# Logits inside the turn of each output tile, routing in separately planned instructions, and a plan with traced durations

## The chip, the cores and the metric

The kernel runs on 1 core of one Trainium2 chip. The metric is the device time of one execution in microseconds (us), as the median of several runs. The profile and the trace are those of one execution, taken by the hardware profiler.

Names of engines: PE is TensorE (PEld its weight loads), DVE is VectorE, ACT is ScalarE, POOL is GpSimd, SP is SyncE, which here only issues DMAs. L12 is line 12 of the kernel before.

## What is computed

Three layers, one after the other, in float32. The first is a gated linear attention with a complex, per-element decay; the second a mixture of 8 experts, of which each token takes one (top-1, with a capacity of 384 per expert); the third a dense FFN with a leaky ReLU. Cut to what matters:

```python
# q, k, v, a_re, a_im: (2, 8, 768, 48); the state S is 48x48 complex per head
for t in range(768):
    S = a[t] * S + outer(k[t], v[t])      # |a| is limited to 0.999
    y[t] = q[t] @ real(S)
x = y as (1536 tokens, 384)

logits = x @ w_gate                        # (1536, 8)
e = argmax(logits); gate = softmax(logits)[e]
slot = number of earlier tokens with the same e    # kept while slot < 384
out = gate * (relu(x @ w1[e]) @ w2[e])     # w1: 8 x 384 x 1024, w2: 8 x 1024 x 384

h = out @ w_in                             # 384 -> 2048
return (max(h, 0) + alpha * min(h, 0)) @ w_out     # 2048 -> 384
```

## The kernel before

**The front part.** The 1536 tokens are 12 tiles of 128. For each tile the decay is brought into log-polar form, summed along the tokens by a matmul with a triangle (`log_polar`, `decay`, `turns`, `edge`), turned back into factors, and multiplied into keys and queries (`rotate`). `attend` (L608 to L740) then works per tile with all 8 heads: it transposes keys and queries, four heads at a time (L628, PSUM tag `tr`, two buffers), copies them out (L633 on ScalarE, L635 on VectorE), forms the scores (L648), masks them on VectorE (L654), and forms the output `y` (L667) and the state update `u` (L681). The output comes out with features on the partitions, two heads of 64 padded rows side by side. ScalarE copies it to `xT` (L701); four transpositions per tile turn it to tokens on the partitions, in a PSUM tile `px` that shares the two `tr` buffers (L706); and ScalarE copies the 48 real columns per head out as the rows `x` (L710).

**Routing.** `route(g)` (L743) works on groups of tiles: `ROUTES` is [0, 1, 2], [3, 4, 5], [6, 7], [8, 9], [10, 11]. For each tile `logit` forms the logits with four matmuls from `xT` and `wg` into a PSUM tile `lg` (L763). `choose` (L774 to L790) is one block of VectorE instructions: the largest logit, its first index, a one-hot row in bf16, the difference to the largest, and, per tile, a copy of the running counts `racc` and an addition to them. `count` (L792) forms the slots with three small bf16 matmuls. `place` (L800 to L823) is a second block: the slot of each token, whether it is over capacity, the index of its row for the scatter (`sidx`) and for the later gather (`gidx`), five instructions that prepare the first FFN tiles (`eidx`), and a part of the gate. GpSimd then scatters the rows to HBM with an indirect DMA per tile (`send`, L840). The last group, [10, 11], is not planned: `first_expert` (L878 to L949) writes its instructions out in order, between warming matmuls (L1112), the product `pa` (L920) that assembles the first expert's tokens without waiting for the scatter of the last tiles, and the halves `xh`, `xl` of it (L939, L940). `finish_routes` (L951) takes the exponentials and finishes the gates.

**The order.** All instructions of the front part but those of `first_expert` are put in order by a planner, `Plan` (L86). Each step has an engine, a cost in us, the values it reads and writes, and PSUM or SBUF buffers that it needs. The planner goes through time, and on each engine takes next what can start earliest, ties by `rank` (a number per kind of step plus the tile's index, table `RANK`) and then by the longest remaining path. `LAG` is added from one step's end to the start of those that depend on it. Steps with `port=True` on VectorE and GpSimd are kept from overlapping each other. Before `COLD` us the planner takes TensorE's steps as `SLOW` times as long; before `EARLY` us DMA issues as `HEAVY` times as long. The order found is fixed per engine; each engine then works it off strictly in turn and waits by semaphores. `choose` and `place` are one step each, with costs of 1.2 + 0.25 n and 1.3 to 2.0 us for n tiles.

**Filling.** Where the plan shows a gap on TensorE longer than `FILL_MIN` ahead of a step that has a `fill`, 0.6 of that gap (`FILL`) is filled with matmuls on the triangle (`keep_warm`, L1110 to L1112), whose result is overwritten. They start once the triangle, part of the load `cst`, has landed.

**Behind the front part** come 8 experts of 256 tokens (`ffn`: `hp` at L1194, `y` at L1177, with each f32 operand split into a high and a low half and three products of these) and the FFN on three chunks of 512 tokens. The splitting of weights (`wh` on ScalarE, `wl` on VectorE) runs beside. Two experts' first weights are split in the front part (L1016, L1020) where the plan finds room.

Of the kernel before, what the change touches and what calls it, by code (L numbers as in the profile page):

```python
# [189 lines left out]
def const_array():  # L190
# [5 lines left out]
    for c in range(2):  # L196
# [4 lines left out]
    io = np.tile(np.arange(NE), (P, GT))  # L201
    c = np.concatenate(
        [tri, tri / (2 * math.pi), last, tri - np.eye(P), cq, ck, io, twin, np.eye(P), np.tile(np.arange(SLOTS), (P, 1))],
# [6 lines left out]
def tile_kernel(  # L210
# [34 lines left out]
    iota = consts[:, CW + P:CW + P + SLOTS]  # L245
    xh0 = cpool.tile([P, DM // P, SLOTS], F32R, name="xh0")
# [112 lines left out]
    wg = acp.tile([P, H // 2, NE], F32, name="wg")  # L359
# [24 lines left out]
    plan = Plan({**RAW, **TMP, "kk": TMP["qq"], "v": 6, "x": 6, "kT": 2, "qT": 2, "pT": 2, "xT": GT, "st": 3, **PS}, ("tr", "sc"))  # L384
# [31 lines left out]
    def load(g, names, cost=0.6):  # L416
        for i in groups[g]:
            for nm in names:
# [9 lines left out]
                plan.op("S", cost, fn, put=[f"{nm}{i}"], new=[(nm, f"{nm}{i}")], lag=2.2)  # L428
# [56 lines left out]
    def decay(i):  # L485
# [6 lines left out]
        tensor(0.65, lambda: T.matmul(out=pl(), lhsT=tri, rhs=tl[f"l{i}"], start=True, stop=True),  # L492
# [7 lines left out]
    def edge(i):  # L500
# [21 lines left out]
        tensor(0.26, turn, use=[e0, "ident"], put=[p], new=[("pc", p)])  # L522
        vector(0.08, lambda: V.tensor_copy(out=ze(), in_=pz()[:, :, 31]), use=[p], put=[f"ze{i}"])
        tensor(0.2, spread, use=[f"ze{i}", "cst"], put=[p])
# [6 lines left out]
    def turns(i):  # L531
# [8 lines left out]
        tensor(0.65, lambda: T.matmul(out=pl(), lhsT=tri_pi, rhs=tl[t], start=True, stop=first),  # L540
               use=[t, "cst"], put=[p], new=[("pc", p)], fill=lambda: pl()[:, 0:P])
        if not first:
            tensor(0.65, lambda: T.matmul(out=pl(), lhsT=last_row, rhs=tl[f"f{i - 1}"], start=False, stop=True),  # L543
                   use=[f"f{i - 1}"], put=[p])
# [63 lines left out]
    def attend(i):  # L608
# [12 lines left out]
        def tr(hh):  # L621
            for src, nm, sc in ((kk, "kT", 1.0 / LAM), (qq, "qT", 1.0)):
# [14 lines left out]
                tensor(0.45, turn, use=[src, "ident"], put=[p], new=[("tr", p), (nm, t)],  # L637
# [22 lines left out]
        def outs(hh):  # L660
            def products():
# [12 lines left out]
                new=[] if hh else [("y", f"y{i}")],  # L674
            )

        def state(hh):
# [8 lines left out]
            tensor(0.7, products, use=[kk, vk], put=[f"u{i}"], new=[] if hh else [("u", f"u{i}")])  # L686
# [13 lines left out]
        def out():  # L700
            A(out=buf(wk, "xT", xk, [P, H // 2, P], GT), in_=y(), func=ACTF.Copy)  # L701

        def back():
            pt = psum("tr", p, [P, H // 2, P])
            for j in range(H // 2):
                T.transpose(pt[:, j, :], tl[xk][:, j, :], ident)  # L706

        def rows():
            xt[i] = xpool.tile([P, DM], F32, tag="x", name="x", bufs=6)
            A(  # L710
                out=xt[i].rearrange("p (h d) -> p h d", d=D),
                in_=tl[p].rearrange("p j (m d) -> p (j m) d", d=HW)[:, :, 0:D], func=ACTF.Copy,
            )
# [29 lines left out]
    def route(g):  # L743
# [8 lines left out]
        def bank(shape, key, tag):  # L752
            return psum(tag if tail else "u", key, shape)

        for j, i in enumerate(tl_):
            x = f"xT{i}"
            if tail:
                plan.rank = i - 1

            def logit(j=j, x=x):  # L760
                pl = bank(shp, f"lg{g}", "sc")
# [116 lines left out]
    def first_expert():  # L878
# [69 lines left out]
        for j in range(n):  # L948
            V.tensor_tensor(out=racc, in0=racc, in1=ohb[:, j], op=ALU.add)  # L949
# [592 lines left out]
```

## Time and profile before

| | us |
|---|---|
| median of 3 runs | 526.89 (525.55 to 528.17) |
| the profiled execution's own time | 525.41 |
| its span, first to last instruction | 523.4 |
| TensorE busy, share of the span | 497.0 (95%) |
| VectorE busy | 352.5 (67%) |
| ScalarE busy | 307.5 (59%) |
| GpSimd busy | 70.1 (13%) |
| first product of the first expert (hp) starts | 166.5 |

A page of the profile gives the busy time of each engine and the chain of work that ended last. The trace behind it can be asked for busy times in chosen stretches, for the chain piece by piece, and for the instructions of an engine in order of time. "Idle before" and "<-" name how long the engine had waited and what released it. Busy time of matmuls is modelled at its end and pieces of one engine can overlap in a listing, so costs are best read from one start to the next. PEclk is the clock that TensorE was granted, as a share of 2.4 GHz.

### The profile page before, as it was taken

How to read it: one execution, taken by the hardware profiler on the slowest of the kernel's cores; microseconds unless marked ns; L12 is line 12 of the kernel's file. 1: busy time of each engine (PE TensorE's matmuls, PEld its weight loads, DVE VectorE, ACT ScalarE, POOL GpSimd, SP SyncE). 2: the span in 40 equal slices, each digit the busy share in tenths (PEclk: the TensorE clock that was granted, in tenths of full speed). 3: DMA queues.
4: the chain of work that ended last, by engine and by line, in shares of the span. 5: the costliest groups of instructions: out<-in, count | busy, mean ns of one | idle time of the engine just before them, and what ended most of it. 6: DMA issues, size and time to landing. Idle time of an engine off the chain costs nothing.

```text
span 523.4 us, 8708 instructions
## 1 busy us (share of the span) xinstructions
PE 497.0 (95%) x3343; PEld 452.6 (86%) x3343; DVE 352.5 (67%) x649; ACT 307.5 (59%) x566; POOL 70.1 (13%) x73
## 2 busy tenths in 40 slices
PE   3689999989999999999999999999999999999994
PEld 2468878878888999999999998899989998999984
DVE  4487999999896677766779958999453433333432
ACT  6697889979753466656665435555453434434441
POOL 0141232425412000120000113000020000000000
PEclk9787999999999999999999999999999999999998
DMA  8543797512033886758975366441021000100002
GB/s 260 193 137 95 258 324 253 185 65 60 33 122 122 311 288 242 241 142 307 317 236 174 123 198 202 161 131 51 1 91 32 0 1 1 61 0 1 0 1 66
DMA packets 37298, 71.76 MB, mean 137 GB/s; under 512 B 3865, under 2 KB 28450, under 8 KB 36482
## 3 DMA queue, kind: packets, MB, share of 16 engines
q1 hardware_dynamic: 35314, 65.93, 38.2%
q0 software_dynamic: 1792, 5.12, 3.0%
q8 instruction: 28, 0.46, 0.4%
q14 instruction: 20, 0.16, 0.1%
q10 hardware_dynamic: 144, 0.10, 0.1%
HBM read 56.56 MB, written 14.56 MB: 136 GB/s over the span
## 4 chain that ended last, share of the span: by engine, by line
PE 89%; DVE 4%; ACT 3%; DMA 1%; issue 1%; SPq 0%; DVEq 0%
PE y L1177 32%; PE hp L1194 32%; PE y L667 3%; PE sc L648 3%; PE pt L540 2%; PE u L681 2%; PE lg L763 2%; PE pqT L628 2%; PE pkT L628 2%; PE pt L543 1%; PE pt L1154 1%; PE pl L492 1%; PE px L706 1%; DMA cst<-in_consts 1%; ACT ar L436 1%; ACT L404 1%
## 5 line engine op out<-in xcount | busy, mean ns | idle before, releaser
L1194 PE MATMUL hp<-xh,wh 128*128 128x256 f32 (+1 forms) x336 | 110.4, 330 | 0.0
L1194 PE MATMUL hp<-xh,wl 128*128 128x256 f32 (+1 forms) x336 | 109.6, 328 | 0.0
L1177 PE MATMUL y<-wh,gh 128*128 128x384 f32 x320 | 108.5, 339 | 0.0
L1177 PE MATMUL y<-wl,gh 128*128 128x384 f32 x320 | 107.7, 337 | 0.0
L1194 PE MATMUL hp<-xl,wh 128*128 128x256 f32 (+1 forms) x336 | 107.1, 329 | 0.0
L1177 PE MATMUL y<-wh,gl 128*128 128x384 f32 x320 | 91.4, 339 | 0.0
L349 DVE TENSOR_TENSOR wl<-st,wh 128x768 fp32r<-128x768 f32 (+1 forms) x63 | 67.5, 1071 | 16.6 <-ACT wh L348 16.2
L1211 DVE SCALAR_TENSOR_TENSOR gn<-gn,nalp,gp 128x512 f32<-128x512 f32 x48 | 36.0, 749 | 63.3 <-ACT gp L1210 63.3
L1209 ACT ACTIVATE gn<-hp 128x512 f32<-128x512 f32 x48 | 28.7, 598 | 80.6 <-PE hp L1194 73.5
L1194 PEld LDWEIGHTS hp<-xh,wh 128*128 128x128 f32 x336 | 63.2, 188 | 5.6 <-ACT xh L1442 0.6
L1194 PEld LDWEIGHTS hp<-xh,wl 128*128 128x128 f32 x336 | 63.2, 188 | 4.4
L1194 PEld LDWEIGHTS hp<-xl,wh 128*128 128x128 f32 x336 | 62.2, 188 | 5.1 <-DVE xl L1443 0.2
L348 ACT ACTIVATE wh<-st 128x768 fp32r<-128x768 f32 (+1 forms) x63 | 58.8, 933 | 6.6 <-DMA st<-in_moe_w 3.7
L1177 PEld LDWEIGHTS y<-wl,gh 128*128 128x128 f32 x320 | 60.2, 188 | 1.5
L1177 PEld LDWEIGHTS y<-wh,gh 128*128 128x128 f32 x320 | 60.2, 188 | 1.4
L1177 PEld LDWEIGHTS y<-wh,gl 128*128 128x128 f32 x320 | 56.9, 188 | 0.8
L1204 ACT ACTIVATE gh<-hp 128x256 fp32r<-128x256 f32 x64 | 24.6, 384 | 49.8 <-PE hp L1194 46.0
L1213 DVE TENSOR_TENSOR gl<-gn,gh 128x512 fp32r<-128x512 f32 x48 | 33.2, 691 | 29.3 <-ACT gh L1212 28.5
L438 POOL TENSOR_TENSOR ai<-ai 128x384 f32<-128x384 f32 x36 | 35.9, 997 | 83.9 <-ACT ai L495 82.0
L1212 ACT ACTIVATE gh<-gn 128x512 fp32r<-128x512 f32 x48 | 30.2, 628 | 19.5 <-DVE gn L1211 18.3
L1205 DVE SCALAR_TENSOR_TENSOR gl<-hp,gh 128x256 fp32r<-128x256 f32 x64 | 26.9, 421 | 14.8 <-ACT gh L1204 14.6
L1210 ACT ACTIVATE gp<-hp 128x512 f32<-128x512 f32 x48 | 28.4, 591 | 0.0
(190 smaller groups left out, 771.3 us busy)
## 6 DMA issues: line engine op xcount, KB each, us to landing
st<-in_moe_w SPq DMA_DIRECT2D x24, 512.0 KB, 5.3
st<-in_moe_w SPq DMA_DIRECT2D x12, 768.0 KB, 4.5
sw<-in_moe_w_in SPq DMA_DIRECT2D x6, 1024.0 KB
sw<-in_moe_w_out SPq DMA_DIRECT2D x8, 768.0 KB, 4.2
xs_d<-zero SPq DMA_DIRECT2D x4, 1152.0 KB, 5.9
vt<-in_v SPq DMA_DIRECT2D x12, 256.0 KB, 5.1
st<-in_moe_w SPq DMA_DIRECT2D x8, 384.0 KB, 3.4
ys_d<-o SPq DMA_DIRECT2D x16, 192.0 KB, 5.2
```

The source lines that it names most:

```text
L348: follow(A(out=wh[:, js], in_=st, func=ACTF.Copy), behind, "A")
L349: follow(V.tensor_tensor(out=wl[:, js], in0=st, in1=wh[:, js].bitcast(F32), op=ALU.subtract), behind, "V")
L438: (V if e == "V" else G).tensor_tensor(out=t, in0=t, in1=t, op=ALU.mult)
L1177: ins = T.matmul(out=ys[t], lhsT=a[:, sl], rhs=b[:, f, :], start=(ft == 0 and m == 0), stop=(ft == nf - 1 and m == 2))
L1194: ins = T.matmul(out=hp, lhsT=a[:, c, fs], rhs=b[:, c, :], start=(n == 0), stop=(n == 3 * KC - 1))
L1204: last["A"] = A(out=gh, in_=hp, func=ACTF.Relu)
L1205: last["V"] = V.scalar_tensor_tensor(out=gl, in0=hp, scalar=0.0, in1=gh.bitcast(F32), op0=ALU.max, op1=ALU.subtract)
L1209: A(out=gn, in_=hp, func=ACTF.Relu, scale=-1.0)
L1210: A(out=gp, in_=hp, func=ACTF.Relu)
L1211: V.scalar_tensor_tensor(out=gn, in0=gn, scalar=nalp[:, ft:ft + 1], in1=gp, op0=ALU.mult, op1=ALU.add)
L1212: last["A"] = A(out=gh, in_=gn, func=ACTF.Copy)
L1213: last["V"] = V.tensor_tensor(out=gl, in0=gn, in1=gh.bitcast(F32), op=ALU.subtract)
```

## The change

- **Logits.** A new load `selw` holds, for each pair of heads, a matrix of 128 rows and 104 columns: 96 columns that pick the real features of the two heads, and 8 columns of `w_gate`. The four transpositions to `px` become four plain matmuls of `xT` with `selw`. The product holds the rows, and for each pair of heads a part of the logits. A VectorE reduction sums the four parts into `lgs`, which keeps the logits of all tiles in SBUF. The 12 x 4 logit matmuls and the PSUM tile `lg` go. `xT` has 2 buffers instead of 3.
- **Routing.** `choose` and `place` are split into 9 VectorE steps and one TensorE step (`count`), planned one by one with a cost of 0.09 us each on VectorE, most with `port=True`. The running counts go; a step `earlier` adds up the one-hot rows of earlier groups (`ohs`), and `count` adds those of earlier tiles of the group by matmuls. The last group uses the same functions. `gidx`, `eidx`, the gates, the differences to the largest logit and the total counts move to `finish_routes`, once for all tiles.
- **The plan.** Costs are changed to durations from a trace, ranks are changed, and `COLD`, `EARLY` and `HEAVY` are lowered. The costs of loads follow their size.
- **Filling.** 20 matmuls on a memset tile stand ahead of all else on TensorE (`first_warm`). Gaps are counted from the end of the first planned step on. 0.85 of a gap is filled; before 55 us gaps from 0.3 us, later from 0.8 us. More steps have a `fill`.

```diff
+NXT = 2
+SELW = 2 * HD + NE
-C_Y = 0.95
-C_ACT, C_BIAS, C_TT, C_STT, C_PS, C_WIDE, C_SQ = 0.415, 0.51, 0.47, 0.5, 0.47, 0.87, 0.79
-LAG = {'A': 0.14, 'V': 0.13, 'G': 0.1, 'T': 0.28, 'S': 2.2}
+C_Y = 1.03
+C_CUM, C_CARRY, C_EDGE, C_STATE, C_TURN = 0.7, 0.7, 0.3, 0.65, 0.445
+C_KB = 1.0 / 290
+C_X = 0.78
+C_SMALL = 0.09
+C_ACT, C_BIAS, C_TT, C_STT, C_PS, C_WIDE, C_SQ = 0.415, 0.51, 0.47, 0.47, 0.47, 0.87, 0.9
+LAG = {'A': 0.14, 'V': 0.13, 'G': 0.1, 'T': 0.28, 'S': 2.4}
-CLEAR_RANK = 3.5
-COLD, SLOW, EARLY, HEAVY = 22.0, 1.9, 22.0, 1.3
+CLEAR_RANK = 3.6
+COLD, SLOW, EARLY, HEAVY = 10.0, 1.9, 0.0, 1.0
-WARM_FROM = 6.0
-FILL, FILL_MIN, FILL_MAX, C_FILL = 0.6, 0.5, 14, 0.23
-RANK = {'L': -6, 'T': -2.5, 'D': -2.2, 'R': -1.3, 'E': -2.1, 'A': -0.3, 'O': 1}
+FILL, FILL_MIN, FILL_LATE, FILL_UNTIL, FILL_MAX, C_FILL = 0.85, 0.3, 0.8, 55.0, 16, 0.235
+WARM_FIRST = 20
+RANK = {'L': -4.96, 'T': -2.81, 'D': -2.3, 'R': -1.16, 'E': -2.21, 'A': -0.63, 'O': 0.92}
...
         def back():
-            pt = psum("tr", p, [P, H // 2, P])
+            pt = psum("tr", p, [P, H // 2, SELW])
             for j in range(H // 2):
-                T.transpose(pt[:, j, :], tl[xk][:, j, :], ident)
+                T.matmul(out=pt[:, j, :], lhsT=tl[xk][:, j, :], rhs=selw[:, j, :], start=True, stop=True)
...
+        def logits():
+            V.tensor_reduce(
+                out=lgs[:, i, :], in_=tl[p][:, :, 2 * D:SELW].rearrange("p j e -> p e j"), axis=AX.X, op=ALU.add
+            )
...
-        tensor(0.45, back, use=[xk, "ident"], put=[p], new=[("tr", p)])
+        tensor(C_X, back, use=[xk, "wg"], put=[p], new=[("tr", p)],
+               fill=lambda: psum("tr", p, [P, H // 2, SELW]).rearrange("p j e -> p (j e)")[:, 0:P])
+        vector(0.1, logits, use=[p], put=[f"lg{i}"])
...
+        if g:
+            vector(0.15, earlier, use=[f"oh{r}" for r in range(g)], put=[f"rb{g}"], port=True)
         if tail:
...
-        vector(1.2 + 0.25 * n, choose, use=[f"lg{g}", "racc", "ready"], put=["racc", f"oc{g}"])
-        tensor(0.3, count, use=[f"oc{g}", "ready"], put=[f"pp{g}"], new=[("u", f"pp{g}")])
-        vector(2.0 if tl_[0] < CHT else 1.3, place, use=[f"pp{g}"], put=[f"si{g}"])
+        vector(C_SMALL, largest, use=[f"lg{i}" for i in tl_], put=[f"mx{g}"], port=True)
+        vector(C_SMALL, equal, use=[f"mx{g}"], put=[c], port=True)
+        vector(C_SMALL, ranks, use=[c, "ready"], put=[c], port=True)
+        vector(C_SMALL, lowest, use=[c], put=[f"cm{g}"], port=True)
+        vector(C_SMALL, hot, use=[c, f"cm{g}"], put=[f"oh{g}"], port=True)
+        tensor(0.3, count, use=[f"oh{g}", "ready"] + ([f"rb{g}"] if g else []), put=[f"pp{g}"], new=[("u", f"pp{g}")])
+        vector(C_SMALL, mine, use=[f"pp{g}", f"oh{g}"], put=[f"om{g}"])
+        vector(C_SMALL, slot, use=[f"om{g}"], put=[f"sl{g}"], port=True)
+        vector(C_SMALL, over, use=[f"sl{g}", f"cm{g}"], put=[f"ok{g}"], port=True)
+        vector(C_SMALL, index, use=[f"ok{g}", f"sl{g}"], put=[f"si{g}"], port=True)
...
     def finish_routes():
-        A(out=dl, in_=dl, func=ACTF.Exp)
+        V.tensor_tensor(out=lgs, in0=lgs, in1=mxs.to_broadcast([P, NTILE, NE]), op=ALU.subtract)
+        A(out=dl, in_=lgs, func=ACTF.Exp)
+        # and gidx, gate, racc and the five instructions for eidx, over all tiles
...
-    sync(0.1, ["wg"], out=wg, in_=w_gate)
+    sync(192 * C_KB, ["wg"], out=selw[:, :, 0:2 * D], in_=picks.unsqueeze(1).to_broadcast([P, H // 2, 2 * D]))
+    sync(0.1, ["wg"], out=selw[:, :, 2 * D:SELW], in_=w_gate)
...
+    def first_warm():
+        by = wk.tile([P, 4, P], F32, tag="pT", name="by", bufs=2)[:, 0]
+        V.memset(by, 1.0)
+        where = ps.tile([P, P], F32, tag="sc", name="warm", bufs=PS["sc"])
+        keep_warm(lambda: where, WARM_FIRST, by)
+
+    emit(first_warm)
+    idle_from = None
     for n in plan.order():
         o = plan.ops[n]
         if o["engine"] == "T":
-            gap = plan.start[n] - max(idle_from, WARM_FROM)
+            gap = plan.start[n] - (plan.start[n] if idle_from is None else idle_from)
             idle_from = plan.start[n] + o["cost"]
-            if o["fill"] is not None and gap > FILL_MIN:
+            if o["fill"] is not None and gap > (FILL_MIN if idle_from < FILL_UNTIL else FILL_LATE):
                 emit(lambda: keep_warm(o["fill"], min(int(FILL * gap / C_FILL), FILL_MAX)))
```

## Rows read from the trace of the kernel before

**Rows 1.** The page: shares of the chain that ended last, by engine.
```profile
PE 89%; DVE 4%; ACT 3%; DMA 1%; issue 1%; SPq 0%; DVEq 0%
```
**Rows 2.** Busy us by stage: length, then PE, PEld, DVE, ACT, POOL; PEclk; DMA.
```profile
17.60:24.20 6.60, 5.88 (x18) 4.14 (x19) 4.59 (x9) 4.03 (x9) 0.06 (x1) 0.50 0.38 119
...
35.00:44.80 9.80, 8.97 (x41) 6.75 (x40) 8.17 (x17) 7.30 (x14) 1.68 (x2) 0.50 0.47 136
44.80:160.00 115.20, 111.62 (x1068) 95.45 (x1067) 105.69 (x244) 92.59 (x175) 39.65 (x39) 1.00 0.46 153
...
166.70:523.40 356.70, 349.55 (x2079) 328.95 (x2078) 216.04 (x330) 179.62 (x324) 19.39 (x17) 0.99 0.38 125
```
**Rows 3.** The chain piece by piece, in the start: start us, us, what.
```profile
8.97 3.78 PE pl L1112 x16
12.76 1.29 PE pl L492 x2
...
14.07 0.49 ACT ar L494
...
18.07 0.52 PE pz L514 x4
```
**Rows 4.** Timelines of VectorE and of ScalarE before the first product.
```profile
9.40 0.55 DVE L478 SCALAR_TENSOR_TENSOR l<-l,w 128x384 f32<-128x384 f32 x1
...
11.35 1.11 ACT L475 ACTIVATE w<-w,bk 128x384 f32<-128x384 f32 x2
```
**Rows 5.** The chain piece by piece: px, logits and warming matmuls.
```profile
37.05 1.11 PE px L706 x4
...
64.86 0.44 PE px L706 x4
...
67.27 0.79 PE lg L763 x8
...
161.85 0.49 PE px L706 x4
...
162.56 1.22 PE warm L1112 x10
```
**Rows 6.** Busy time, summed over the stretches of the eight routing blocks.
```profile
sum 17.88, PE 15.97 PEld 13.37 DVE 15.97 ACT 13.67 POOL 8.16; mean PE 2.00 PEld 1.67 DVE 2.00 ACT 1.71 POOL 1.02
```
**Rows 7.** Timeline of VectorE in the first routing block.
```profile
69.64 0.18 DVE L779 TENSOR_REDUCE mx<-lg 128x3 f32<-128x24 f32 x1 [0.16 <-PE lg L763]
69.86 0.18 DVE L780 TENSOR_TENSOR cand<-lg,mx 128x24 f32<-128x24 f32 x1
...
72.20 0.67 DVE L790 TENSOR_TENSOR racc<-racc,ohb 128x8 f32<-128x8 f32 x1
```
**Rows 8.** Busy time by stretch, as rows 2, around the first two groups' routing.
```profile
70.00:80.00 10.00, 8.18 (x80) 6.84 (x80) 9.45 (x30) 7.44 (x17) 6.25 (x7) 1.00 0.95 346
100.00:110.00 10.00, 8.54 (x79) 7.10 (x78) 9.04 (x34) 8.73 (x17) 4.42 (x4) 1.00 0.29 85
```
**Rows 9.** Timeline of VectorE in the tail: its reader of px.
```profile
163.28 0.56 DVE L908 TENSOR_TENSOR al<-px,ah 128x384 fp32r<-128x384 f32 x1 [0.38 <-ACT x L710]
```
**Rows 10.** Timelines of VectorE and TensorE as the first expert begins.
```profile
167.47 0.17 DVE L943 TENSOR_TENSOR dl<-lg,mx 128x16 f32<-128x16 f32 x1
...
168.10 0.25 DVE L954 TENSOR_REDUCE sm<-dl 128x12 f32<-128x96 f32 x1
...
168.94 0.42 DVE L1205 SCALAR_TENSOR_TENSOR gl<-hp,gh 128x256 fp32r<-128x256 f32 x1
...
170.68 0.51 PE L1177 MATMUL y<-wh,gl 128*128 128x384 f32 x2
```
**Rows 11.** Timeline of SP's queue.
```profile
27.60 8.99 SPq L426 DMA_DIRECT2D vt<-in_v  x2
```
**Rows 12.** Timelines of TensorE and VectorE: one score product and its mask.
```profile
70.35 1.06 PE L648 MATMUL sc<-qT,kT 96*128 96x128 f32 x8
...
73.80 0.68 DVE L654 TENSOR_TENSOR pT<-sc,cst 128x512 f32<-128x512 f32 x1
```

More of the change, by code (lines that the diff above doesn't have):

```diff
@@ L201, in const_array @@
     io = np.tile(np.arange(NE), (P, GT))
+    sel = np.zeros((P, 2 * HD))
+    for m in range(2):
+        sel[m * HW:m * HW + HD, m * HD:(m + 1) * HD] = np.eye(HD)
     c = np.concatenate(
-        [tri, tri / (2 * math.pi), last, tri - np.eye(P), cq, ck, io, twin, np.eye(P), np.tile(np.arange(SLOTS), (P, 1))],
+        [tri, tri / (2 * math.pi), last, tri - np.eye(P), cq, ck, io, twin, np.eye(P), np.tile(np.arange(SLOTS), (P, 1)), sel],
         axis=1,
@@ L750, in route @@
         st = {}
[L752 to L761, printed above, removed]
-                for c in range(H // 2):
-                    st["lg"] = T.matmul(
-                        out=pl[:, j, :], lhsT=tl[x][:, c, :], rhs=wg[:, c, :], start=(c == 0), stop=(c == H // 2 - 1)
-                    )
-            tensor(
-                0.9, logit, use=[x, "wg"], put=[f"lg{g}"], new=[] if j else [("sc" if tail else "u", f"lg{g}")]
-            )
@@ new lines, in lowest, with hot, earlier @@
+        def lowest():
+            V.tensor_reduce(out=cms[:, tsl], in_=st["cand"], axis=AX.X, op=ALU.min)
+        def hot():
+            V.tensor_tensor(out=ohs[:, tsl], in0=st["cand"], in1=shared(cms), op=ALU.is_equal)
+        def earlier():
+            st["rb"] = small("rb", [P, 1, NE], BF16)
+            with nc.allow_low_precision("counts up to the number of tiles"):
+                V.tensor_reduce(
+                    out=st["rb"].rearrange("p o e -> p (o e)"), in_=ohs[:, 0:tl_[0]].rearrange("p n e -> p e n"),
+                    axis=AX.X, op=ALU.add,
+                )
@@ new lines, in count, with mine @@
+            for b in range(n - 1):
+                T.matmul(
+                    out=pp[:, b + 1:n, :], lhsT=onesb,
+                    rhs=ohs[:, tl_[0] + b:tl_[0] + b + 1].to_broadcast([P, n - 1 - b, NE]), start=False, stop=False,
+                    skip_group_check=True,
+                )
+            T.matmul(out=pp, lhsT=strib, rhs=ohs[:, tsl], start=False, stop=True)
+        def mine():
+            st["oh"] = small("oh")
+            V.tensor_tensor(out=st["oh"], in0=st["pp"], in1=ohs[:, tsl], op=ALU.mult)
@@ L823, in place @@
-            V.tensor_scalar(out=gate[:, tsl], in0=ok.rearrange(col), scalar1=-1.0, scalar2=1.0, op0=ALU.mult, op1=ALU.add)
+                out=sidx[:, tsl], in0=oks[:, tsl].rearrange(col), scalar=65536.0, in1=sls[:, tsl].rearrange(col),
+                op0=ALU.mult, op1=ALU.add,
+            )
+        chain = dict(
+            largest=largest, equal=equal, ranks=ranks, lowest=lowest, hot=hot, count=count, mine=mine, slot=slot, over=over,
+            index=index,
+        )
+        if g:
+            vector(0.15, earlier, use=[f"oh{r}" for r in range(g)], put=[f"rb{g}"], port=True)
@@ L824, in route @@
         if tail:
-            ends.update(st, tl=tl_, n=n, shp=shp, tsl=tsl, logits=lambda: bank(shp, f"lg{g}", "sc"), small=small)
+            ends.update(chain, st=st, tl=tl_, n=n, tsl=tsl)
             return
-        vector(1.2 + 0.25 * n, choose, use=[f"lg{g}", "racc", "ready"], put=["racc", f"oc{g}"])
-        tensor(0.3, count, use=[f"oc{g}", "ready"], put=[f"pp{g}"], new=[("u", f"pp{g}")])
-        vector(2.0 if tl_[0] < CHT else 1.3, place, use=[f"pp{g}"], put=[f"si{g}"])
+        c = f"ca{g}"
```

181 lines of the change are left out of this document (76 added, 105 removed).

## The prediction

> **What bounds the kernel now.** I read the chain of waits first, then a table of busy time by stage, then the chain again piece by piece, and last the timelines of the stretches in which TensorE waits. The chain ends in TensorE for 89% of the span [rows 1]. The stages [rows 2] say what that means: the expert and FFN part, from 166.70 us to the end, has TensorE busy 349.55 of 356.70 us, and the change leaves its matmuls alone. So what the change does is decided by when that part begins. Before it lie a start, in which TensorE twice drops to the lower of its two clocks (granted 0.50, that is 1.2 GHz, from 17.60 to 24.20 us and from 35.00 to 44.80 us), a dense middle from 44.80 to 160.00 us (TensorE 111.62, VectorE 105.69, ScalarE 92.59 of 115.20 us), and a tail of 6.7 us. In the middle the chain goes through TensorE nearly everywhere, one product after the other. TensorE and VectorE are both above 90% there, so a saving on one of them alone need not pay; this change takes work from both.
>
> **The sum** is made for the profiled execution: 525.41 us, of which 523.4 us are span. The median of the runs is 526.89 us, 1.48 us more, and I add that at the end.
>
> **Start (A).** Three places can gain.
> (a) TensorE begins at 8.97 us with 16 filling passes, 236 ns each, and the first real product runs after them, at 12.76 us [rows 3]. Its input was ready at 9.40 + 0.55 = 9.95 us [rows 4]. The change fills from a memset tile instead, from about 1 us on: 20 matmuls of two passes each are 40 x 0.236 = 9.4 us at that pace, so they end by 10.5 us, and the first product is planned with no fill ahead of it. It would end at 10.5 + 1.29 = 11.8 us instead of 14.05 us. ScalarE, which reads it at 14.07 us [rows 3], is busy with other tiles until 11.35 + 1.11 = 12.46 us [rows 4]. If its order stays, the gain is 14.07 - 12.46 = 1.6 us; 2.8 us if the planner reorders. I take 1.6.
> (b) From 17.60 to 24.20 us TensorE is busy 5.88 of 6.60 us at half clock. With the fills the idle 4.0 us before it (14.05 to 18.07 us [rows 3]) hold matmuls, and the clock has a reason to stay up. Then 2.9 us of its work vanish; but VectorE is busy 4.59 us in the same stretch [rows 2], so I allow only 6.60 - 4.59 = 2.0 us.
> (c) From 35.00 to 44.80 us likewise: TensorE 8.97 us at half clock, up to 4.5 us to save; VectorE busy 8.17 of 9.80 us allows 1.6 us.
> Together 5.2 us. Upper bound, if VectorE's work moves elsewhere: 2.8 + 2.9 + 4.5 = 10.2 us. Lower bound below nothing: fills are sized for full clock (0.235 us each, 85% of the planned gap). Should the clock stay low, they take twice that, 1.7 gaps, and a 4.0 us gap costs 0.7 x 4.0 = 2.8 us.
>
> **Middle (B), TensorE.** Each tile today costs one transposition back, 0.44 us, and four logit matmuls in 8 passes, 0.79 us [rows 5]. Afterwards it is one plain matmul per pair of heads, again 8 passes with 128 rows of weights, but 104 columns. No row has 104 columns. The logit pass with 8 columns takes 0.79/8 = 99 ns, the warm fill of 128 columns 1.22/10 = 122 ns [rows 5]; 8 passes are 0.79 to 0.98 us. I take 0.85, since 8 columns already cost four fifths of 128, so that columns weigh little. In the middle fall 11 tiles' logits and 10 transpositions: 11 x 0.79 + 10 x 0.44 = 13.1 us go and 10 x 0.85 = 8.5 us come, 4.6 us saved (3.3 to 5.2).
> **VectorE.** The routing of the four planned groups stands in eight unbroken blocks, 17.88 us from their first instruction to their last in all [rows 6]; part of that is small instructions that swell from 0.18 to 0.67 us [rows 7]. Afterwards each group needs 9 small instructions on VectorE, at 0.22 us from one to the next that depends on it (69.64 to 69.86 us [rows 7], and so on in these blocks): 4 x 9 x 0.22 = 7.9 us. To these come 11 logit sums (the twelfth falls in the tail) and 3 sums of earlier groups, bounded by 0.18 us, the reduce that opens the first block [rows 7], and 0.25 us, the largest reduce in the end of routing [rows 10]; at 0.2 they are 2.8 us. So 17.9 - 10.7 = 7.2 us are freed, and no block is longer than one instruction. TensorE waits exactly there: it is busy only 8.18 and 8.54 us in the two tens of microseconds that hold the first two groups' routing [rows 8], which is 3.3 us of idling. I take half of it as gained, 1.6 us, since the instructions still have to run.
> 4.6 + 1.6 = 6.2 us. VectorE would then have 105.7 - 7.2 = 98.5 us to do in 109, 90%, and ScalarE 85%, which leaves little slack, so I take four fifths: 5.0 us. Bounds 0 and 8 (6.2 and the other half of the idling).
>
> **A new reader of the product (px).** ScalarE copies the rows out of it, and now VectorE sums the logits out of it. In the tail VectorE's subtraction, which reads this product too, began only when ScalarE's second copy of it had ended, 0.38 us later than its inputs needed [rows 9]. So the two may read one after the other. The Trainium skill, page PSUM — Partial Sum Buffer, section PSUM bank collisions raise a hardware error, says that two engines must not read one bank at the same time and that the order has to be kept by dependencies; this row agrees, and by that rule each tile's sum or copy waits for the other. The wait costs up to one copy, 0.49 us by ScalarE's other reads of TensorE's products (0.49 at 14.07 us [rows 3]); 11 x 0.49 = 5.4 us. In my forecast that hides, since ScalarE has 22.6 us idle in the middle; if it doesn't, B is gone. That is a rival below.
>
> **Tail (C).** The logits come from the product itself, so 0.49 us of TensorE go before the warming matmuls; the logit sum puts 0.2 us into VectorE's chain. Net 0.3 us gained (-0.3 to 0.6).
>
> **End of routing (D).** It runs as the FFN begins: 9 instructions from 167.47 to 168.94 us, then the first gl, done at about 169.4 us, which TensorE needs at 170.68 us [rows 10]. It grows to 13 instructions, 0.8 to 1.0 us more, against a cover of 1.3 us. The cover is nearly used up, so I charge 0.3 us (0 to 1.0).
>
> **Nothing** for the loads: the selection matrix is 192 KB more on SP's queue, and w_gate lands in 32-byte pieces. They are issued just ahead of a pair of loads that hold the queue for 8.99 us [rows 11], because these wait for a buffer; that covers them. The reader, px of tile 0, runs at 37.05 us [rows 5]. Without that cover they would cost about 1 us. The setup swaps one tiny memset for one tiny product.
>
> Sum: 5.2 + 5.0 + 0.3 - 0.3 = 10.2 us. 525.41 - 10.2 = 515.2, and 1.5 more against the median: **516.7 us**.
>
> **Rivals.**
> R1, the clock falls as before. The fills don't reach far enough, or ScalarE's chain at 14 to 18 us holds the start anyway; A is 0. For it: the first product waits for ScalarE and table loads, not for TensorE. 526.9 - 5.0 = 521.9 us.
> R2, B is swallowed by the two readers of px and by VectorE's strict order: only A pays. For it: three engines above 80% in the middle, and the row of the 0.38 us. 526.9 - 5.2 = 521.7 us.
> R3, both: about 526.9 us.
> R4, slower: px stays occupied. It shares two PSUM buffers (tag tr) with the four transpositions of each tile, and is now freed only when VectorE, too, has come to it. VectorE's backlog can be long: a score product that ends at 71.24 us is masked at 73.80 us, 2.6 us later [rows 12]. If the next transposition stands behind that on TensorE for 1.3 us more per tile, 11 tiles cost 14.3 us against the gain of 10.2: 526.9 + 4.1 = 531.0 us. The point from which it decides is 10.2/11 = 0.93 us per tile. Against it: that backlog is one of routing blocks, which are taken apart, and the planner knows the buffer.
>
> **How the numbers follow.** Forecast 0.50, R1 0.20, R2 0.12, R3 0.08, R4 0.10. The first three are faster by over 0.5% (2.6 us, about what a measurement here can tell from no change), less a little for the smaller ends of R1 and R2: 0.80. Same: 0.10. Slower: 0.10. The forecast's own range follows from the bounds, 508.5 (A 10.2, B 8, C 0.6, D 0, nearly all at once) to about 522. To 527 it takes in R1, R2 and half of R3; R4, the rest of R3 and a little at the low end stay out: 508 to 527.
>
> **What would show it.** A: granted clock 1.00 from 17.6 to 24.2 us and 35 to 44.8 us, first product before 12 us. B: px at 0.85 us per tile and no lg; the span from one px to the next at about 10.2 us (today 97.0 us for the nine from 64.86 to 161.85 us, 10.8 each [rows 5]); no ten microseconds in the middle with TensorE under 9. D: first gl before 170.7 us counted from a first hp at 166.7 us. Wrong would be a granted clock of 0.50 in the start (R1), TensorE idle behind VectorE or ScalarE reading px (R2), or transpositions waiting for the logit sum (R4). The FFN part must stay at 356.7 us within 1 us; if it doesn't, weights came late, which no step here allows for.

## The result and the profile after

The changed kernel takes 514.07 us (median; 513.62 to 514.42) beside 527.53 us of the kernel before in the same runs: 0.9749 of it, interval 0.9716 to 0.9781. The forecast was 516.7 us in a range of 508 to 527. The profiled execution of the changed kernel takes 513.75 us, 511.6 us of them span.

First the page of the changed kernel: the chain that ended last, to set beside [rows 1].

```profile
PE 86%; ACT 7%; DVE 2%; DMA 2%; issue 1%; POOL 0%; SPq 0%; POOLq 0%
```

Then the busy time by stage (length, PE, PEld, DVE, ACT, POOL, granted clock, DMA share, GB/s), to set beside [rows 2].

```profile
0.00:9.00 9.00, 7.20 (x40) 7.01 (x40) 3.75 (x11) 5.77 (x11) 1.09 (x6) 1.00 0.74 235
17.60:24.20 6.60, 6.47 (x40) 5.06 (x41) 5.70 (x13) 5.87 (x12) 0.00 (x0) 1.00 0.79 235
35.00:44.80 9.80, 9.37 (x79) 7.23 (x79) 9.39 (x16) 8.07 (x16) 0.01 (x1) 1.00 0.45 133
44.80:150.00 105.20, 104.07 (x995) 88.34 (x994) 91.38 (x209) 88.70 (x168) 44.75 (x40) 1.00 0.50 166
153.30:511.60 358.30, 350.18 (x2081) 329.10 (x2079) 215.72 (x324) 179.62 (x324) 18.92 (x18) 1.00 0.38 124
```

The two stretches that stood at 0.50 now stand at 1.00. VectorE fell to 87% of the middle. TensorE is busy 104.07 of 105.20 us there, 98.9%, where it was 96.9%, and idles a little over 1 us. But filling passes count as busy, and this stretch holds 22 of them, where the stretch of before held none (its ten warming matmuls come later, at 162.56 us [rows 5]). Ten of the 22 are these same warming matmuls. The other twelve are new:

```profile
73.43 0.85 PE L1129 MATMUL pz<-cst 128*96 128x128 f32 x6
146.88 0.94 PE L1129 MATMUL px<-cst 128*128 128x128 f32 x6
```

They stand where TensorE would have waited: the products behind them start at 74.23 and 147.65 us, some 0.05 us after ScalarE's instructions of that moment end (ar at 74.18, xT at 147.59 us). So they cover 0.80 and 0.77 us of waiting.

Three marks divide the execution in every kernel of this study: the first px (the turn of tile 0), the first hp (the FFN begins), and the end of the span. For the kernel before the timeline of TensorE puts px at 37.05 us [rows 5] and hp at 166.52 us. These are the px and hp of the changed kernel (start us, us, engine, line, op, tiles):

```profile
32.74 1.14 PE L724 MATMUL px<-selw,xT 128*128 128x104 f32 x8
48.34 1.09 PE L724 MATMUL px<-selw,xT 128*128 128x104 f32 x8
153.32 0.28 PE L1218 MATMUL hp<-xh,wh 128*128 128x256 f32 x1
```

So 4.3 us were gained up to the first px, 8.9 us from there to hp (129.47 against 120.58 us), and 1.4 us lost after it (356.88 against 358.28 us): 11.8 us of span. Of the 8.9 us, 2.4 lie between the first and the second px (18.0 against 15.6 us), where the kernel before ran at the lower clock. The other 6.5 us come after the second px. Here are the stretches from there to hp, of before and then of after:

```profile
55.04:166.52 111.48, 107.21 (x1029) 92.71 (x1028) 100.49 (x244) 85.73 (x160) 38.82 (x38) 1.00 0.49 163
```
```profile
48.34:153.32 104.98, 103.85 (x986) 88.67 (x986) 91.64 (x222) 85.96 (x162) 42.87 (x38) 1.00 0.50 166
```

TensorE is busy 3.4 us less (107.21 to 103.85) and idles 3.1 us less (4.27 to 1.13). With the 1.6 us of the twelve new filling passes counted as waiting, it has 4.9 us less to do, and its waiting falls by 1.6 us, from 4.3 to 2.7 us. What it had waited for in before, and waits for in after, the view of waits says for the same stretches (who waited, for whom, us in all, times, longest):

```profile
PE y L667 <- DVE pT L654: 1.2, 2, 0.7
PE pz L518 <- DVE ze L523: 1.0, 1, 1.0
PE pp L797 <- DVE ocb L789: 1.0, 1, 1.0
PE lg L763 <- ACT xT L701: 0.7, 1, 0.7
```
```profile
PE pqT L645 <- DVE lgs L731: 0.4, 1, 0.4
PE px L724 <- ACT qT L650: 0.2, 1, 0.2
```

Waits for VectorE made up 3.2 us of the rows of before, the wait of the slots' product pp for the routing block (ocb) among them; that one is gone. The timeline of VectorE in the first group's routing, to set beside [rows 7], shows how the block was taken apart: between its small instructions stand those of other tiles.

```profile
66.33 0.17 DVE L781 TENSOR_REDUCE mxs<-lgs 128x3 f32<-128x24 f32 x1
66.42 0.55 DVE L471 TENSOR_TENSOR t<-t,ai 128x384 f32<-128x384 f32 x1
66.88 0.18 DVE L785 TENSOR_TENSOR cand<-lgs,mxs 128x24 f32<-128x24 f32 x1
66.98 0.61 DVE L615 SCALAR_TENSOR_TENSOR ai<-k,cst,ai 128x384 f32<-128x384 f32 x1
```

### The profile page after: what moved, and what is told of

Read it like the earlier page. It is cut to its first block, busy times and chain, and to the rows that moved or that the text cites. A ratio compares the mean times of both kernels' runs of the same rounds, so it can differ in the third digit from the quotient of the medians.

```text
span 511.6 us, 8770 instructions
## 1 busy us (share of the span) xinstructions
PE 497.2 (97%) x3386; PEld 453.6 (89%) x3386; DVE 343.3 (67%) x622; ACT 307.0 (60%) x566; POOL 74.2 (15%) x73
## 4 chain that ended last, share of the span: by engine, by line
PE 86%; ACT 7%; DVE 2%; DMA 2%; issue 1%; POOL 0%; SPq 0%; POOLq 0%
PE hp L1218 32%; PE y L1201 32%; PE y L684 4%; PE sc L665 4%; PE u L698 2%; PE px L724 2%; PE pkT L645 2%; PE pt L1178 1%; PE pqT L645 1%; PE pt L557 1%; PE pl L506 1%; PE pt L560 1%; DMA sw<-in_moe_w_out 1%; ACT L418 1%; DMA ar<-in_a_re 1%
## 5 line engine op out<-in xcount | busy, mean ns | idle before, releaser
L452 POOL TENSOR_TENSOR ai<-ai 128x384 f32<-128x384 f32 x36 | 33.6, 933 | 65.6 <-ACT ai L509 63.7
```

The lines of the kernel that those rows point to most:

```text
L452: (V if e == "V" else G).tensor_tensor(out=t, in0=t, in1=t, op=ALU.mult)
```

## Experiments

The two theories. **One price:** TensorE sets the pace, so the fold of the logits pays by the TensorE time that it removes, and the split of the routing pays only by the idling that it ends. **The order:** what VectorE's blocks and the planner's order do to the queues decides, and TensorE time that is saved pays only where nothing else is late. All kernels stand in this table. The ratio is to the kernel before in the same runs; the other columns are us of each profiled execution. Between kernels that were not run together, a difference of medians and one of ratios can be 1.5 us apart, so both are given where it matters.

| kernel | ratio (interval) | first px | px to hp | hp to end |
|---|---|---|---|---|
| before | 1 | 37.05 | 129.5 | 356.9 |
| changed | 0.9749 (0.9716–0.9781) | 32.74 | 120.6 | 358.3 |
| a_again (the changed kernel once more) | 0.9765 (0.9723–0.9807) | 32.82 | 120.6 | 357.6 |
| a_oldfill | 0.9839 (0.9805–0.9873) | 37.95 | 120.5 | 356.8 |
| a_oldrank | 0.9816 (0.9762–0.9870) | 34.52 | 122.5 | 358.0 |
| a_oldplan | 0.9879 (0.9837–0.9922) | 34.06 | 126.3 | 357.6 |
| a_blocks | 0.9860 (0.9817–0.9902) | 32.86 | 126.4 | 359.5 |
| a_gates | 0.9757 (0.9722–0.9791) | 32.98 | 120.5 | 358.4 |
| a_px_twice | 0.9945 (0.9926–0.9963) | 33.28 | 130.8 | 356.6 |
| a_dve_more | 0.9865 (0.9811–0.9919) | 33.12 | 126.4 | 358.2 |
| b_newfill | 0.9947 (0.9924–0.9970) | 35.13 | 129.3 | 356.9 |
| b_newplan_fill | 0.9921 (0.9898–0.9945) | 33.24 | 130.1 | 358.7 |
| b_logits_newplan_fill | 0.9954 (0.9926–0.9981) | 33.03 | 132.7 | 356.6 |
| b_logits | 1.0157 (1.0121–1.0194) | 37.08 | 137.7 | 357.0 |

### The fills alone, from both sides

a_oldfill is the changed kernel with the fills of before, in the same planned order; b_newfill is the kernel before with the new fills.

```diff
-FILL, FILL_MIN, FILL_LATE, FILL_UNTIL, FILL_MAX, C_FILL = 0.85, 0.3, 0.8, 55.0, 16, 0.235
+FILL, FILL_MIN, FILL_MAX, C_FILL = 0.6, 0.5, 14, 0.23
...
-    emit(first_warm)
-    idle_from = None
+    idle_from = 0.0
```

> The changed kernel with the fills of the kernel before (no matmuls ahead of the first load, the old constants, the old steps with a fill); the planned order is the changed kernel's. Theory 1 (the start's gain is the clock): the granted clock falls to 0.50 again in the first 45 us, and the time rises by 4 to 6 us, to 518 to 520 us. Theory 2 (the start is held by ScalarE and VectorE, and the new order is what gained): the clock may fall, but the time rises by less than 2 us, to at most 516 us.

> The kernel before with the fills of the changed kernel and nothing else; its planned order is the old one. Theory 1: the clock stays at 1.00 from about 8 us on, and the time falls by 3 to 6 us, to 521.5 to 524.5 us. Theory 2: within 1.5 us of the kernel before (526 to 529 us), since the old order was made for a slow TensorE in the first 22 us and the other engines hold it.

a_oldfill took 517.27 us, 3.2 more than the changed kernel (4.7 by the ratios), between what the two theories expected. Its first px comes 5.2 us later and the way from px to hp is the same 120.5 us, so up to hp the fills act on the stretch before the first px and nowhere else in this order; behind hp it is 1.5 us shorter than the changed kernel (see below). The granted clock column did not fall in the first 45 us, as theory 1 had expected, but the pace was low: two passes of pt at 24.31 us took 1.14 us to the next start, two like them at 28.40 us took 0.65. The timeline of TensorE in a_oldfill shows the place of (a) and (b) in the prediction, the first product behind 16 fills and then 4 us of nothing:

```profile
9.22 3.78 PE L1128 MATMUL pl<-cst 128*128 128x128 f32 x16 [9.22 <-DMA cst<-in_consts]
12.79 1.49 PE L507 MATMUL pl<-l,cst 128*128 128x384 f32 x2
18.31 0.52 PE L529 MATMUL pz<-ident,ar 32*96 32x32 f32 x4 [4.03 <-ACT ar L451]
```

In the changed kernel the first product and that turn stand at

```profile
10.16 0.91 PE L506 MATMUL pl<-l,cst 128*128 128x384 f32 x2 [1.80 <-DVE l L492]
15.80 0.37 PE L528 MATMUL pz<-ident,ar 32*96 32x32 f32 x4 [1.23 <-ACT ar L450]
```

that is, 2.6 and 2.5 us earlier. In b_newfill the same fills gained 1.9 us at the first px and 5.6 at the second (49.41 us), but only 2.1 were left at hp. Its 523.62 us are 3.0 less than before, as theory 1 expected, but the clock did not stay up: it is 0.74 from 17.6 to 24.2 us. What was lost behind the second px is 3.6 us: TensorE idles 5.3 us there instead of 4.3, and from 100 to 110 us the granted clock is 0.83, which is some 3.4 us at half pace and by estimate 1.7 us lost. That the other parts of the change would have prevented this isn't shown.

### TensorE's price: the turn twice

a_px_twice computes every px a second time, in the same order; nothing else changes.

```diff
-            for j in range(H // 2):
-                T.matmul(out=pt[:, j, :], lhsT=tl[xk][:, j, :], rhs=selw[:, j, :], start=True, stop=True)
+            for _ in range(2):
+                for j in range(H // 2):
+                    T.matmul(out=pt[:, j, :], lhsT=tl[xk][:, j, :], rhs=selw[:, j, :], start=True, stop=True)
```

> The changed kernel with each tile's product px formed twice, 8 more passes of TensorE per tile, unknown to the planner. The product costs 0.79 to 0.98 us by the trace. Theory 1 (TensorE bounds the middle, so its work counts one for one): 12 times 0.8 to 0.95, that is 9.5 to 11.5 us more, 523.5 to 525.5 us. Theory 2 (VectorE and ScalarE bound the middle as much): less than half of it, under 5 us more, below 519 us.

It took 522.88 us, 8.8 more than the changed kernel (10.3 by the ratios), 0.6 us under what theory 1 expected and far above theory 2. From px to hp it is 10.3 us longer, 0.86 us for each of the twelve turns. Pieces of the chain in the changed kernel give the price of one turn, from its start to the next product's, as 0.93 (at 141.40 us) to 0.97 us, not 0.85:

```profile
48.50 0.94 PE px L724 x8
...
147.81 0.97 PE px L724 x8
```

Twelve more turns at 0.93 us are 11.2 us of work, of which 10.3 show at hp: in this order TensorE's time counts nearly one for one.

### VectorE's price: nine more small instructions a group

a_dve_more puts nine redundant operations behind the index of each planned group, unknown to the planner, in the same order.

```diff
+            if not tail:
+                for _ in range(9):
+                    V.tensor_tensor(out=st["oh"], in0=st["oh"], in1=st["oh"], op=ALU.max)
```

> The changed kernel in the same order, with nine more small VectorE instructions behind the index of each of the four planned groups, 4 x 9 x 0.2 = 7 us of work that the planner doesn't know of and that changes no value. Theory 1, VectorE sets the pace of the middle together with TensorE: 3 to 6 us longer up to the first hp. Theory 2, VectorE has slack there and only TensorE counts: under 1.5 us.

It is 1.2% slower than the changed kernel by the ratios (0.9865 against 0.9749), 6 us, and from px to hp 5.8 us longer. The 36 instructions take 159 to 219 ns each, 178 at the median, 6.4 us in all. So VectorE's time, put in as unbroken blocks of 1.9 us, counts nearly one for one too, though VectorE is busy only 87% of the middle. How much of that is the time itself and how much that it comes in blocks, this run can't tell. TensorE now waits where it had not:

```profile
PE pl L506 <- DVE t L471: 1.4, 1, 1.4
PE y L684 <- DVE pT L671: 1.2, 1, 1.2
PE y L684 <- DVE Z L755: 0.9, 1, 0.9
```

These waits lie in three places, each behind another of the four blocks: the products start at 77.73, 108.98 and 134.04 us, 2.5 to 3.0 us after a block of nine began. The 3.5 us in these rows are not all of the 5.8; in the middle as a whole (44.8 us to 157 us) TensorE idles 5.3 us, 4.2 more than in a_again up to 151 us.

### The fold alone

b_logits is the kernel before with the logits taken from the turn and nothing else (routing in its two blocks, old fills, old plan constants; the order is planned anew).

```diff
-            pt = psum("tr", p, [P, H // 2, P])
+            pt = psum("tr", p, [P, H // 2, SELW])
             for j in range(H // 2):
-                T.transpose(pt[:, j, :], tl[xk][:, j, :], ident)
+                T.matmul(out=pt[:, j, :], lhsT=tl[xk][:, j, :], rhs=selw[:, j, :], start=True, stop=True)
...
+        vector(0.1, logits, use=[p], put=[f"lg{i}"])
```

> The kernel before with the logits inside the turn of the tile alone (selw, the sum on VectorE, two xT buffers); routing in its two blocks, constants, ranks and fills of the kernel before. Theory 1: 4.6 us of TensorE saved in the middle show as 3 to 5 us, 522.5 to 524.5 us. Theory 2 (another reader of px and 12 more instructions on a full VectorE take it back): within 1.5 us of the kernel before, 526 to 529 us.

533.8 us, 7.2 us slower than before. Neither expectation held. From px to hp it takes 8.3 us longer, though TensorE has less to do. Of these, 3.3 us lie between the first and the second px (21.25 against 18.0 us), ahead of all routing, and 5.0 us behind it. The view of waits from px to hp:

```profile
PE pp L790 <- DVE ocb L782: 2.2, 1, 2.2
PE sc L654 <- DVE qT L641: 1.8, 1, 1.8
PE px L712 <- ACT xT L707: 1.7, 3, 0.9
PE u L687 <- DVE Z L735: 1.5, 1, 1.5
```

and the place of the first of them, on TensorE's timeline, with the busy time of that ten microseconds:

```profile
79.55 0.18 PE L787 MATMUL pp<-base,onesb 1*128 1x24 bf16 x1
81.97 0.17 PE L790 MATMUL pp<-ocb,onesb 128*128 128x24 bf16 x1 [2.24 <-DVE ocb L782]
...
83.17 3.41 PE L654 MATMUL sc<-qT,kT 96*128 96x128 f32 x16
```
```profile
80.00:90.00 10.00, 8.03 (x56) 7.36 (x56) 8.79 (x28) 7.66 (x12) 4.92 (x6) 0.83 0.85 283
```

The slots' product reached the head of TensorE's queue 2.2 us before the routing block was done, everything behind it stood, and the granted clock fell on top: sixteen score products at 213 ns each, where eight take 1.06 us in [rows 12], 133 ns each. But this is one of three places where the clock fell, as the ten microseconds around the others show:

```profile
50.00:60.00 10.00, 8.52 (x86) 7.48 (x85) 7.64 (x15) 8.03 (x16) 4.54 (x6) 0.94 0.42 143
60.00:70.00 10.00, 10.00 (x82) 7.98 (x81) 9.45 (x21) 8.61 (x17) 0.00 (x0) 0.89 0.85 280
160.00:170.00 10.00, 7.46 (x68) 6.80 (x67) 5.18 (x7) 1.37 (x3) 3.19 (x5) 0.83 0.41 134
```

At each of the three TensorE ran at the lower clock for some 3.4 us (0.06 and 0.11 of ten us, doubled; 0.17, doubled, at the other two), which by estimate costs 1.7 us each time, 5.1 in all: as much as this kernel loses behind the second px. Only the place at 80 us stands behind the routing block. The first follows TensorE's wait of 1.5 us for Z, which came behind a product qq of 1.58 us on VectorE, the last its wait of 1.8 us for qT, behind 2.16 us of splitting weights (wl). None of these waits is for the new reader of px. Whether px, held for a second reader, made the planner find this worse order stays open.

### Old and new plan, and the fold under the new plan

a_oldplan is the changed kernel with all constants of the old plan (costs, lags, ranks, start); a_oldrank with the old table of ranks alone. b_newplan_fill is the kernel before with the new constants and fills; b_logits_newplan_fill adds the fold to that.

```diff
-LAG = {'A': 0.14, 'V': 0.13, 'G': 0.1, 'T': 0.28, 'S': 2.4}
+LAG = {'A': 0.14, 'V': 0.13, 'G': 0.1, 'T': 0.28, 'S': 2.2}
...
-COLD, SLOW, EARLY, HEAVY = 10.0, 1.9, 0.0, 1.0
+COLD, SLOW, EARLY, HEAVY = 22.0, 1.9, 22.0, 1.3
...
-RANK = {'L': -4.96, 'T': -2.81, 'D': -2.3, 'R': -1.16, 'E': -2.21, 'A': -0.63, 'O': 0.92}
+RANK = {'L': -6, 'T': -2.5, 'D': -2.2, 'R': -1.3, 'E': -2.1, 'A': -0.3, 'O': 1}
```

> The changed kernel with the planner's costs, lags, ranks and start-up constants of the kernel before; code, logits, split routing and fills as changed. Theory 1 (the gain is the clock, TensorE's work and VectorE's freed time): under 3 us lost, at most 517 us. Theory 2 (the order found is what pays, and work taken away pays only under it): 5 us or more lost, 519 us or above.

> The changed kernel with only the old table of ranks (the priorities by which the planner picks among what is ready). The old plan constants together cost 6.3 us. Theory 1, the traced costs and lags carry that: 0 to 2 us above the changed kernel. Theory 2, the ranks carry it: 4 to 6.5 us above.

> The kernel before with the new fills and the new constants of the plan (costs, lags, ranks, start), its routing and logits untouched. New fills alone gave 523.62 us. Theory 1, the traced costs make a better order for any code: 516 to 521 us, since the old constants cost the changed kernel 6.3 us. Theory 2, the constants are good only together with the changed instructions: 523 to 526 us.

> The same kernel plus the fold of the logits into the turn, with routing still in its two blocks. The fold takes 12 x 0.79 us of logit products off TensorE and adds about 12 x 0.45 us. Theory 1, TensorE sets the middle's pace: 3 to 4.5 us less than without the fold in this batch, and what is left to the changed kernel (514 us) is worth of the split of routing, 2 to 5 us. Theory 2, the fold itself costs by holding the product's PSUM buffers for VectorE, as the slower kernel with the fold alone suggested: 2 us or more above the one without it.

The old constants cost the changed kernel 6.3 us (520.07 us beside 513.81 of a_again), as theory 2 expected, the old ranks alone 0.7% by the ratios, 3.5 us, between what the two expected, so neither the ranks nor the costs carry it alone. The same constants gave the kernel before next to nothing beyond its fills: 0.9921 after 0.9947, with the intervals overlapping. So they paid only together with the changed instructions, as theory 2 of that run expected. Why is not shown. Each kernel here is one order that the planner found, and no run repeats a part under several orders; the ranks, numbers of two decimals, may suit this one kernel.

Under the new constants the fold, with the routing still in its blocks, is 1.4 us slower than without it (524.44 beside 523.07 us in the same runs, intervals overlapping), though it takes 12 x (0.79 + 0.44 - 0.93) = 3.6 us off TensorE: slower, but by less than theory 2 expected. From px to hp it is 2.6 us longer, 1.3 of them before the second px (15.6 against 14.3 us). From the second px to hp TensorE idles 8.0 us beside 5.8 and runs 42 filling passes beside 26, at 0.12 us or more each. That makes about 4 us more of waiting, idle or filled, against the 3.6 us saved. TensorE's timeline in b_logits_newplan_fill shows one such place:

```profile
98.14 0.18 PE L794 MATMUL pp<-base,onesb 1*128 1x24 bf16 x1
99.75 0.17 PE L797 MATMUL pp<-ocb,onesb 128*128 128x24 bf16 x1 [1.43 <-DVE ocb L789]
...
100.56 0.66 PE L678 MATMUL y<-pT,vt 128*64 128x128 f32 x8 [0.60 <-DVE pT L665]
```

and the stretches around it what came after:

```profile
97.50:100.00 2.50, 1.02 (x13) 0.70 (x11) 2.26 (x11) 2.47 (x5) 1.10 (x2) 1.00 0.00 0
100.00:102.00 2.00, 1.21 (x13) 0.90 (x13) 2.00 (x5) 1.14 (x3) 0.00 (x0) 0.79 0.00 0
102.00:104.00 2.00, 2.00 (x11) 2.00 (x11) 1.73 (x14) 1.20 (x4) 0.59 (x1) 0.50 0.38 102
104.00:107.00 3.00, 3.00 (x8) 1.73 (x9) 2.39 (x6) 0.89 (x2) 2.70 (x2) 0.50 0.18 66
107.00:110.00 3.00, 3.00 (x24) 2.71 (x23) 1.62 (x4) 0.61 (x1) 1.32 (x2) 0.84 0.35 131
```

TensorE was busy 1.02 of 2.50 us and 1.21 of 2.00 us, and then worked at 1.2 GHz for some 6.8 us (0.8 from the second row, 5.0, 1.0 from the last), which by estimate costs half of that, 3.4 us. b_newplan_fill has a like place at 100 to 107 us, with about 3.4 us at the lower clock, 1.7 us lost. That difference is 1.7 of the 2.6 us.

### Routing in two blocks

a_blocks is the changed kernel with the nine VectorE instructions of a group planned as two blocks, `choose` and `place`, but without what the change put off to the end of routing.

```diff
-        vector(C_SMALL, largest, use=[f"lg{i}" for i in tl_], put=[f"mx{g}"], port=True)
...
-        vector(C_SMALL, index, use=[f"ok{g}", f"sl{g}"], put=[f"si{g}"], port=True)
+        vector(1.1, choose, use=[f"lg{i}" for i in tl_] + ["ready"], put=[c, f"oh{g}"], port=True)
...
+        vector(0.88, place, use=[f"pp{g}", f"oh{g}"], put=[f"si{g}"], port=True)
```

> The changed kernel with the nine routing instructions of a group planned as two unbroken blocks of five and four; the planner orders anew. Theory 1 (unbroken blocks made TensorE wait): 1.5 to 4 us lost, 515.5 to 518 us. Theory 2 (shorter routing is the gain, its splitting is not): within 1 us of the changed kernel, 513 to 515 us.

519.28 us, 5.5 more than a_again, and 5.8 us more from px to hp, all of it behind the second px; more than was expected of it. From the second px to hp TensorE idles 3.9 us where the changed kernel idles 1.1, and runs 42 filling passes where that runs 22, so about 5.2 of the 5.8 us are waiting, idle or filled. But it isn't the slots' product that waits: pp is in no row of the view of waits. The longest wait there before the tail is a filled px behind VectorE's qT:

```profile
PE px L1130 <- DVE qT L652: 0.8, 1, 0.8
```

In this order the blocks cost by pushing back VectorE's other work, for which the planner then left gaps on TensorE. Step by step from px to hp: 130.1 us with the old routing, 132.7 with the fold, 126.4 with what is put off to the end taken out of the blocks, 120.6 with the blocks split. Each step plans a new order, so a step is the part together with the order that the planner found for it; a_oldplan shows that the order alone is worth as much as a step. No run takes the fold out of the changed kernel, so what the fold is worth once the blocks are split is argued from the price of a turn, not measured.

### After hp

a_again runs the changed kernel once more; a_gates forms the gate products of the last expert's first tiles one block later.

```diff
-            hooks[FT - 1 - CHT + j].append(lambda behind, j=j: first_chunk_gates(behind, j))
+            hooks[FT - CHT + j].append(lambda behind, j=j: first_chunk_gates(behind, j))
```

> The changed kernel once more, for a second trace. In the first trace the part from the first product of the first expert to the end took 358.3 us against 356.9 us before, with TensorE waiting 0.9 us behind gathers of the last expert. Theory 1 (the longer end of routing costs it in every execution): 358 us again. Theory 2 (the gathers started 2 us late in that one execution): 356.6 to 357.2 us.

> The changed kernel with the four gate products of the last expert's gathered rows one block later in VectorE's order, so that the split of a block doesn't stand behind a gather. If TensorE's 0.9 us wait there is in every execution, 0.9 to 1.3 us less, 512.8 to 513.2 us; if it is of one execution only, within 0.5 us of the changed kernel.

The place of the loss is on VectorE's timeline of the changed kernel, near the end of the experts: a gate product waits 2.96 us for a gather, and gl comes behind it, which TensorE waits for.

```profile
290.28 0.42 DVE L1423 TENSOR_SCALAR rows<-rows,gate 128x384 f32<-128x384 f32 x1 [2.96 <-DMA rows<-ys_d,eidx]
291.64 0.66 DVE L1423 TENSOR_SCALAR rows<-rows,gate 128x384 f32<-128x384 f32 x1 [0.94 <-DMA rows<-ys_d,eidx]
293.08 0.41 DVE L1229 SCALAR_TENSOR_TENSOR gl<-hp,gh 128x256 fp32r<-128x256 f32 x1
```
```profile
293.55 0.62 PE L1201 MATMUL y<-wh,gl 128*128 128x384 f32 x2 [0.92 <-DVE gl L1229]
```

The first of these gathers starts 133.8 us after the first hp; in before it is 131.8, in a_again 133.2. Moving the products away took no time off (513.64 us, the same as a_again): the wait went to the next expert input instead (0.7 us of hp for xl). The part behind hp took 357.6 us in a_again, between the two expectations. And the loss is not in every kernel with this code behind hp: a_oldfill and a_px_twice take 356.8 and 356.6 us, their gathers start 132.1 and 131.9 us after hp, and TensorE waits for none of them. Why the gathers come 1.4 to 2 us later after hp in the others stays open.

## Why the prediction was right

**Start (A), 5.2 us: right in kind, a little low.** The clock rows, the first product and the first px bear it out. What was gained by the second px is 6.7 us (55.04 to 48.34). The fills alone account for 5.2 us at the first px (37.95 in a_oldfill to 32.74 us), and the new order for the rest: with the old fills the way from the first to the second px was already 15.6 us, so in this order the stretch of step (c) does without the new fills, and its gain comes with the order. The first product ended at 11.1 us, not 11.8, and ScalarE read it at 11.82 us, before the bound of 12.46 us, because the planner put another order there. R1 did not happen. The old fills show a part of it: in the changed order they bring the low pace back up to 25 us, but not in step (c), and cost 3.2 us (4.7 by the ratios).

**Middle (B) with tail (C), 5.3 us: 1.2 us low, which is the fifth taken off for want of slack.** From the second px to hp 6.5 us were gained, and the sum ahead of that discount was 6.2 us. TensorE's part was sized with 0.85 us a turn; it measured 0.93 to 0.97, which makes 13.1 - 9.3 = 3.8 us of the 4.6. The half of the idling, 1.6 us, came out: the column of idle time says 3.1 us, but with the new filling passes counted as waiting it is 1.6. The 1 us that is left over between these 5.4 us and the 6.5 is not traced; the two stretches don't hold quite the same products (128 passes of u before, 122 after). The marks of the forecast came out, too: from px to px it is 9.9 us (nine from 58.99 to 147.65 us), and no ten microseconds have TensorE under 9 (9.47 at the least, fills included).

What the forecast had wrong here is to price the two halves side by side, as if each could be had alone. The fold gained nothing under either plan while the routing stood in its blocks: under the new constants TensorE's waiting grew by about as much as its work fell. VectorE does 8.9 us less from the second px to hp (100.49 to 91.64), where the sum had 7.2 us freed and no price for them by themselves; a_dve_more, which puts 6.4 us back, loses 5.8. So the gain stands on both parts, and on the order that was found for them.

The total, 10.2 us of span forecast and 11.8 measured, is closer than its parts: A was 1.5 us low, the middle 1.2 low, and D 1.1 high. That these partly cancel is luck.

**The new reader of px (R2), at most 5.4 us, was hidden**, as the forecast said. In the middle ScalarE waits 2.6 us for the sum and VectorE 1.6 us for the copy:

```profile
ACT x L728 <- DVE lgs L731: 2.6, 4, 1.6
DVE lgs L731 <- ACT x L728: 1.6, 5, 0.4
```

Most of the 2.6 us is waiting for the product itself, since the sum takes only 0.19 us. But the two do read in turn: in none of the eleven turns from 48 to 153 us do their reads overlap, and in ten of them the second read starts within 0.05 us of the end of the first. By the Trainium skill, page PSUM — Partial Sum Buffer, section PSUM bank collisions raise a hardware error, two engines' reads of one bank must be kept apart; the trace agrees. What reached TensorE is 0.4 us: a transposition, pqT, waited for the sum lgs, which is the wait that R4 feared, in small.

**R4, slower, was a right worry with another cause.** The fold alone is slower by 7.2 us. The prediction laid such a loss to px held in its two buffers, and no wait of b_logits is for that. Its rows show waits for VectorE, one of them the slots' product's for the routing block, and three falls of the clock. What R4 took as its safeguard, that the blocks are taken apart, is what the change gains by: a_blocks loses 5.8 us without it, in its own order.

**Tail (C), 0.3 us: no gain.** From the last y to the first hp it is 6.40 us before and 6.37 after. **End of routing (D), -0.3 us: wrong in place.** Its instructions were put between those of the first expert; the first gl stands at 155.27 us and TensorE's need at 157.5, so it cost nothing there. The 1.4 us (0.7 in a_again) appeared 140 us later, behind the gathers, and not at all in a_oldfill and a_px_twice, so they are not shown to be a price of the longer end of routing. The prediction's mark for it was the FFN part within 1 us of 356.7: one execution is 1.6 us above that and the other 0.9. The mark was read as weights that come late; the rows show gathered tokens.

## What to carry to other kernels

When two engines are both nearly full, measure the price of each by adding work in place and in the same order: here 11 us more on TensorE cost 10 up to the FFN, and 6.4 us on VectorE, in four blocks, cost 6, so neither was the bound by itself. Work taken off one of them can turn into waiting for the other: with the routing in blocks the fold took 3.6 us off TensorE, and its waiting grew by about 4. When reading a busy share, count filling passes as waiting. And count a planner's new order as a part of the change, by running the old constants with the new code and the new constants with the old code.

## What the runs showed of the hardware

The granted clock column read 1.00 for 0 to 9 us of the changed kernel, though its 40 filling passes took 7.20 us, 180 ns each, where the same passes take 122 ns in the tail of before [rows 5]. a_oldfill reads 1.00 from 0 to 45 us, though its filling passes at 9.22 us took 236 ns each and its products ran at half pace until about 25 us. So durations of passes, not the column, tell the pace at the start of these two. In b_logits_newplan_fill the clock fell to 1.2 GHz after TensorE had been busy 2.2 of 4.5 us, with no single wait above 1.43 us, and came back some 6.8 us later. A pass of 104 columns with 128 rows took 116 to 121 ns (0.93 to 0.97 us for eight), closer to the 122 ns of 128 columns than to the 99 ns of 8.
